# Weight conversion from float64 words: the sign bits as a 16-bit operation into ScalarE's word, and the opening lists re-laid

## Chip, core and metric

The kernel runs on one core of a Trainium2 chip. The metric is the device time of one execution, in microseconds (us). The engines that matter here are TensorE (PE in the profile, PEld for its weight loads), VectorE (DVE), ScalarE (ACT) and the SP queue, which issues every DMA.

## The reference

An attention between 512 tokens and 32 state rows per head is followed by a feed-forward layer over 4608 rows. The two weight matrices arrive as float64, the rest as float32.

```python
scores = scale * np.matmul(x, state.transpose(0, 1, 3, 2))      # B, H, S, Ns, D = 8, 8, 512, 32, 64
a = softmax(scores); xread = np.matmul(a, state)
scores2 = scale * np.matmul(state, x.transpose(0, 1, 3, 2))
a2 = softmax(scores2); sread = np.matmul(a2, x)
x = concat([xread, sread], axis=2) -> (4608, 512)
h = x @ w_in            # 512 x 2048, float64
g = h - np.tanh(h)
return (g @ w_out).astype(np.float32)      # 2048 x 512, float64
```

## The kernel before

The weights are loaded as pairs of 32-bit words and turned into float32 on the chip. `Weight.steps` (L142) makes four steps of a block of 128x512: step 0 on DVE takes the upper word, shifts it left by 3 and masks it (L151); step 1 on DVE ORs the two top bits of the upper word into it, a two-source operation (L152); step 2 on ACT scales the lower word by 2^-29 to an integer `r` (L154); step 3 on DVE adds the two integers (L155). There are 32 blocks: 8 column blocks and 8 quarter blocks of `w_in`, and 16 row blocks of `w_out`.

Sixteen of the blocks belong to the opening. There every engine follows a list written out by hand (`lines`, L897), one token per step: a letter for the operation (`ops`, L861) and a number for its block. Letters a, b, r, p are steps 0, 1, 2, 3 of a `w_in` column block; u, v, w, y are the same of a `w_out` block. S is a score product, c its copy out of PSUM on ACT, T its transpose on DVE, M, B, E, Z, I, J, N, A the rest of the softmax (maximum, subtraction, exponential, sum, epsilon, reciprocal, product, transpose back). m is the product of a `w_in` block with the state, k and R its copies on ACT, e a second product of that kind, h and H the two halves of a hidden block of the first two batches, X its tanh (ACT), L the subtraction (DVE), G and g its high and low part, O and Q the output products. D is a blank matmul that computes nothing that is used. A token starts after the one ahead of it on its engine and after the tokens it needs: h needs A0, H needs A1 for the first pair, m needs p, e needs T and c of both halves.

Behind the opening the steps `convert_win` and `convert_wout` (L569, L274) run the other 16 blocks, gated behind the tanh steps, with an order that the framework's scheduler plans from its own costs. `r` lies in a tile of 512 integers with two buffers (tag "cr" for `w_in`, "s" for `w_out` in the opening).

The loads stand in one list on the SP queue (L609 to L620): head, xT, the first `w_in` block w00d, xT, half of `sps`, the second block w01d, the other half of `sps`, `sp4`, and behind them two halves of xT for the third score product and the rest of the weights. The first token, a0, needs w00d; the first state product, m0, needs p0 and both halves of `sps`.

Of the kernel before, what the change touches and what calls it, by code (L numbers as in the profile page):

```python
# [8 lines left out]
F32 = mybir.dt.float32  # L9
F32R = mybir.dt.float32r  # L10
U32 = mybir.dt.uint32
I32 = mybir.dt.int32
ALU = mybir.AluOpType
AF = mybir.ActivationFunctionType
# [28 lines left out]
def attention_ffn(ctx: ExitStack, tc: tile.TileContext, early, xT, xn, bh, sm, sl, win, wout, xout, sout):  # L43
# [10 lines left out]
    nc = tc.nc  # L54
# [71 lines left out]
    class Weight:  # L126
# [5 lines left out]
        def load(self):  # L132
            if self.src.dtype == F32:
                self.raw = next(raws)(f"{self.name}d", [P, 512], F32)
                dst = self.raw
            else:
                self.raw = next(raws)(f"{self.name}d", [P, 512, 2], U32)
                dst = self.raw.rearrange("p f w -> p (f w)")
            src = self.src.bitcast(dst.dtype)
            loadlog.append(nc.sync.dma_start(dst, src).ins)  # L140

        def steps(self, dst, tag="cr"):  # L142

            if self.src.dtype == F32:
                return [lambda: None] * 3 + [lambda: nc.gpsimd.tensor_copy(dst, self.raw)]
            low, high = self.raw[:, :, 0], self.raw[:, :, 1]
            u, i = dst.bitcast(U32), dst.bitcast(I32)
            r = pool.tile([P, 512], I32, tag=tag, name=f"{self.name}r", bufs=CB)
            return [

                lambda: nc.vector.tensor_scalar(u, high, 3, 0x3FFFFFFF, ALU.logical_shift_left, ALU.bitwise_and),  # L151
                lambda: nc.vector.scalar_tensor_tensor(u, high, 0xC0000000, u, ALU.bitwise_and, ALU.bitwise_or),  # L152

                lambda: nc.scalar.activation(r, low, AF.Copy, scale=2.0**-29),  # L154
                lambda: nc.vector.tensor_add(i, i, r),  # L155
            ]

        def convert(self, dst):
            for step in self.steps(dst):
                step()  # L160


    SCH = json.loads('{"conv": [8, 8, 9, 9, 11, 11, 12, 12], "pair": [10, 10, 13, 13], "a0": [96, 97], "att2": [12, 13, 13, 23, 27, 28, 29], "att3": [36, 39, 40, 41, 43, 44, 45, 49, 50], "att4": [49, 53, 53, 55, 57, 59, 60], "att5": [70, 73, 74, 75, 76, 78, 79, 83, 84], "att6": [83, 86, 87, 88, 90, 91, 92], "att7": [102, 105, 106, 107, 108, 110, 111, 116, 117], "m0": [19, 19, 19, 22, 22, 22, 22, 25, 25, 28, 28, 28, 30, 30, 30, 36], "m1": [50, 51, 54, 58, 61, 62, 67, 68, 77, 80, 82, 85], "wo": [8, 12, 12, 13, 13, 16, 19, 22], "r1": [99, 100, 103, 104], "at0": [10, 16], "plain": [1, 5, 6, 7]}')
# [390 lines left out]
    def advance(units, n=1):  # L554
# [7 lines left out]
    w0 = [  # L562
        [Weight(win[4 * q + r], f"w0{4 * q + r}" if q < 2 else f"w{q}{r}") for r in range(4)]
        for q in range(NQ)
    ]
# [75 lines left out]
    def rows(q, j):  # L641
        return q[:, :, (j % 4) * P : (j % 4) * P + P]
# [73 lines left out]
    def win_step(n):  # L716
        def run(j):
            if j not in csteps:
                if j // 2 not in wb:
                    tag, bufs = ("wf", WB) if j < 4 else (f"mr1{j // 2}", 1)  # L720
                    wb[j // 2] = pool.tile([P, 2, 512], F32, tag=tag, name=f"w00{j}", bufs=bufs)
                csteps[j] = wcols[j].steps(wb[j // 2][:, j % 2], "cr")
            csteps[j][n]()
            if n == 3:
                nc.sync.dma_start(rows(wf[j // 4], j), wb[j // 2][:, j % 2].rearrange("p (r f) -> p r f", r=4))
        return run

    def wout_step(n):
        def run(f):
            if f not in wsteps:  # L730
                if f < WHOLE_ROWS:
                    if f % 2 == 0:
                        whole.append(pool.tile([P, 2, 512], F32, tag=("mr", "stage")[f // 2], name=f"wor{f}", bufs=(RRB, SB)[f // 2]))
                    worows[f] = whole[f // 2][:, f % 2]
                else:
                    worows[f] = pool.tile([P, 512], F32, tag="wor", name=f"wor{f}", bufs=RB)
                wsteps[f] = wos[f].steps(worows[f], "s")
            wsteps[f][n]()
            if n == 3:
                with ExitStack() as gates:  # L740
                    for x in stores:
                        gates.enter_context(tc.issue_after(x))
                    load(int(f < len(ring)))
        return run
# [32 lines left out]
    def keep(k):  # L777
        def run(j):
            nc.scalar.copy(m_both[j // 4][:, k, :, (j % 4) * P : (j % 4) * P + P], mps[j][k][:, :2])
        return run  # L780
# [77 lines left out]
    def halt(t):  # L858
# [4 lines left out]
        "W": (late_scores, "S"), "U": (late_turn, "TW"),  # L863
        "B": (sub_max, "M"), "E": (exp, "B"), "Z": (sums, "E"), "I": (add_eps, "Z"),
        "J": (invert, "I"), "N": (normalize, "J"), "A": (turn_back, "N"),
        "a": (win_step(0), ""), "b": (win_step(1), "a"), "r": (win_step(2), ""), "p": (win_step(3), "br"),
        "u": (wout_step(0), ""), "v": (wout_step(1), "u"), "w": (wout_step(2), ""), "y": (wout_step(3), "vw"),
        "i": (wout_high, "y"), "l": (wout_low, "i"), "m": (product, "p"), "k": (keep(0), "m"), "R": (keep(1), "m"),
        "h": (hidden_half(0), "k"), "H": (hidden_half(1), "hR"), "X": (tanh, "H"), "L": (sub_tanh, "X"),
        "G": (g_high, "L"), "g": (g_low, "G"), "O": (output_part((0, 1)), ""), "Q": (output_part((2, 3)), "O"),  # L870
# [19 lines left out]
    for j in range(2, 8):  # L890
        more[f"r{j}"] = f"p{j - 2}"
        more[f"w{j}"] = f"y{j - 2}"
        if j - 2 >= WHOLE_ROWS:
# [2 lines left out]

    lines = {  # L897
        "PE": (
            "D0 D0 D0 S0 W0 D0 D0 D0 D0 S1 D0 D0 m0 e0 D0 D0 m1 S2 h0 h1 H0 e1 H1 m2 O0 h2 Q0 H2 O1 m3 Q1 h3 "
            "O2 H3 m4 Q2 h4 m5 H4 O3 h5 Q3 H5 m6 O4 h6 Q4 H6 O5 m7 Q5 h7 O6 H7 Q6 h8 h9 H8 O7 H9 Q7"  # L900
        ),
        "DVE": (
# [4 lines left out]
        ),  # L907
        "ACT": (
# [3 lines left out]
        ),  # L912
# [23 lines left out]
    a0 = state_read(0, [ss[0], ss[1]])  # L936
# [3 lines left out]
    m1 = [m_units(g) for g in range(2)]  # L940
# [7 lines left out]
    steps = [(0, f) for f in range(HALF)] + [(1, f) for f in range(NFF)] + [(0, f) for f in range(HALF, NFF)]  # L948
    steps += [(i, f) for i in range(2, B + 1) for f in range(NFF)]
    for st, (i, f) in list(enumerate(steps))[HALF:]:  # L950
        with ExitStack() as gates:
            for x in tanhs[st + (st < 2 * NFF)]:
# [8 lines left out]
        if st + LAG < len(steps):  # L961
            ni, nf = steps[st + LAG]
            if nf % 4 == 0:
                if (ni, nf) == (B, 0):
                    advance(turn)
                with ExitStack() as gates:
                    for x in tanhs[st + 1] if st < 2 * NFF else ():
                        gates.enter_context(tc.issue_after(x))
                    chunks[ni].prepare(nf // 4, tanhs[st - 2] if st >= 2 * NFF else ())
            chunks[ni].hidden(nf)  # L970
# [6 lines left out]
        with ExitStack() as gates:  # L977
# [6 lines left out]
            for b in range(2, B):  # L984
                n = SCH[f"att{b}"].count(st)
# [67 lines left out]
```

## Time and profile before

| what | us |
|---|---|
| median of 3 runs (lowest to highest) | 641.0 (640.27 to 641.15) |
| the profiled execution's own time | 641.2 |
| span of the core in that execution | 639.4 |
| PE busy | 634.3 |
| DVE busy | 440.3 |
| ACT busy | 347.6 |

The span is what the trace covers; the execution takes 1.8 us more, which lies around it. Busy times are sums over an engine's instructions, and the instructions of one engine overlap by their start-up, so an engine that is busy for the whole of a stretch has no idle time in it, and the step from one start to the next is shorter than an instruction's duration.

### The profile page before, as it was taken

The page shows a single profiled execution, that of the slowest core. Times are in us where ns is not written, and L with a number is a line of the kernel's source. Part 1 is how long each engine was busy: PE and PEld are TensorE (multiplying, and loading weights), DVE is VectorE, ACT ScalarE, POOL GpSimd, SP SyncE. Part 2 cuts the span into 40 slices and gives each one's busy share as a digit, 9 for nine tenths or more (in the row PEclk, how much of TensorE's full clock was granted, in tenths as well). Part 3 has the DMA queues.
Part 4 walks back from the last instruction along what each step waited for, and adds up shares of the span by engine and source line. Part 5 has one row for each costly group of instructions (what it writes and reads, how often), then busy time and mean ns, then how long its engine had stood idle before and what let it go on. Part 6 is the DMA issues. An engine that isn't in the chain of part 4 may idle for free.

```text
span 639.4 us, 10251 instructions
## 1 busy us (share of the span) xinstructions
PE 634.3 (99%) x3828; PEld 504.8 (79%) x3828; DVE 440.3 (69%) x757; ACT 347.6 (54%) x630; POOL 0.3 (0%) x5
## 2 busy tenths in 40 slices
PE   8999999999999999999999999999999999999998
PEld 5456867888888788878888788878888788888897
DVE  6999999898683874688553686486664875453442
ACT  4865768777674543756553466445543453342442
POOL 0000000000000000000000000000000000000000
PEclk9999999999999999999999999999999999999999
DMA  8993889267886335543533236773361233221400
GB/s 318 401 319 134 281 290 351 85 207 238 261 264 182 104 98 199 174 136 118 171 115 111 83 95 202 251 288 94 121 198 46 79 108 124 76 66 34 133 33 34
DMA packets 66738, 105.87 MB, mean 166 GB/s; under 512 B 12288, under 2 KB 32640, under 8 KB 66688
## 3 DMA queue, kind: packets, MB, share of 16 engines
q1 hardware_dynamic: 66688, 105.21, 50.2%
q8 instruction: 30, 0.49, 0.3%
q14 instruction: 20, 0.16, 0.1%
HBM read 69.01 MB, written 35.65 MB: 164 GB/s over the span
## 4 chain that ended last, share of the span: by engine, by line
PE 97%; DVE 1%; DMA 1%; issue 0%; SPq 0%; ACT 0%
PE ops L519 19%; PE ops L520 19%; PE ops L521 19%; PE hps L472 10%; PE hps L473 9%; PE hps L474 9%; PE hps L812 3%; PE mps L219 2%; PE mps L756 1%; PE rps L410 1%; PE ops L838 1%; PE mps L218 1%; DMA w00d<-in_win 1%; PE sps L287 1%; DVE w L155 0%; DVE z L696 0%
## 5 line engine op out<-in xcount | busy, mean ns | idle before, releaser
L519 PE MATMUL ops<-wo,g 128*128 128x512 f32 x534 | 211.9, 399 | 0.0
L520 PE MATMUL ops<-wo,g 128*128 128x512 f32 x534 | 208.2, 390 | 0.0
L521 PE MATMUL ops<-wo,g 128*128 128x512 f32 x534 | 198.0, 390 | 0.0
L480 DVE TENSOR_TENSOR t<-hps,t 128x512 f32<-128x512 f32 (+1 forms) x134 | 87.7, 656 | 114.6 <-ACT t L480 114.1
L480 ACT ACTIVATE t<-hps 128x512 f32<-128x512 f32 (+1 forms) x134 | 76.5, 573 | 145.3 <-PE hps L474 144.4
L519 PEld LDWEIGHTS ops<-wo,g 128*128 128x128 f32 x534 | 100.2, 188 | 26.9 <-issue 4.2
L520 PEld LDWEIGHTS ops<-wo,g 128*128 128x128 f32 x534 | 100.3, 188 | 22.6 <-issue 2.3
L521 PEld LDWEIGHTS ops<-wo,g 128*128 128x128 f32 x534 | 100.0, 188 | 21.8 <-DVE t L480 0.8
L124 DVE TENSOR_TENSOR g<-t,g 128x512 fp32r<-128x512 f32 (+1 forms) x134 | 87.4, 656 | 32.4 <-ACT g L123 30.3
L123 ACT CAST g<-t 128x512 fp32r<-128x512 f32 (+1 forms) x134 | 79.7, 596 | 48.9 <-DVE t L480 40.4
L472 PE MATMUL hps<-aT,m 128*128 128x512 f32 x232 | 90.7, 391 | 0.0
L473 PE MATMUL hps<-aT,m 128*128 128x512 f32 x232 | 90.4, 390 | 0.0
L474 PE MATMUL hps<-aT,m 128*128 128x512 f32 x232 | 89.8, 389 | 0.0
L472 PEld LDWEIGHTS hps<-aT,m 128*128 128x128 f32 x232 | 43.5, 188 | 10.8 <-DVE wor L151 0.8
L473 PEld LDWEIGHTS hps<-aT,m 128*128 128x128 f32 x232 | 43.6, 188 | 9.6 <-issue 0.8
L474 PEld LDWEIGHTS hps<-aT,m 128*128 128x128 f32 x232 | 43.5, 188 | 9.1
L124 DVE TENSOR_TENSOR wst<-w,wst 64x512 fp32r<-64x512 f32 (+1 forms) x56 | 36.3, 648 | 4.7 <-ACT wst L123 3.1
L124 DVE TENSOR_TENSOR m<-mr,m 128x1024 fp32r<-128x1024 f32 x29 | 35.4, 1222 | 6.0 <-ACT m L123 5.6
L123 ACT CAST m<-mr 128x1024 fp32r<-128x1024 f32 x29 | 30.4, 1047 | 8.8 <-DVE mr L252 5.7
L220 ACT COPY st<-mps 128x512 f32<-128x512 f32 (+1 forms) x56 | 29.9, 558 | 8.7 <-PE mps L219 4.2
L123 ACT CAST wst<-w 64x512 fp32r<-64x512 f32 (+1 forms) x56 | 32.8, 586 | 0.7
L812 PE MATMUL hps<-at,mr 128*128 128x512 f32 x40 | 20.1, 600 | 0.1
(237 smaller groups left out, 588.0 us busy)
## 6 DMA issues: line engine op xcount, KB each, us to landing
md<-st SPq DMA_DIRECT2D x96, 128.0 KB, 2.8
mr<-md SPq DMA_DIRECT2D x20, 512.0 KB, 4.2
xn<-in_xn SPq DMA_DIRECT2D x16, 512.0 KB, 6.0
out_x<-ob SPq DMA_DIRECT2D x30, 256.0 KB, 2.7
xT<-in_xT SPq DMA_DIRECT2D x12, 512.0 KB, 4.7
w<-wf SPq DMA_DIRECT2D x12, 512.0 KB, 4.7
pd<-pe SPq DMA_DIRECT2D x16, 256.0 KB, 2.1
p2t<-pd SPq DMA_DIRECT2D x64, 64.0 KB, 2.0
```

Of the source, the lines that this page charges most:

```text
L123: nc.scalar.copy(hi, src)
L124: return (sub or nc.vector).tensor_sub(lo, src, hi)
L219: nc.tensor.matmul(ps, s[:, 0, h], t[:, e], start=(g == 1), stop=True)
L220: nc.scalar.copy(stage[:, e], ps)
L472: nc.tensor.matmul(ps, mhi[k][:, cols], ahi[:, k], start=(k == 0), stop=False)
L473: nc.tensor.matmul(ps, mhi[k][:, cols], alo[:, k], start=False, stop=False)
L474: nc.tensor.matmul(ps, mlo[k][:, cols], ahi[:, k], start=False, stop=(k == nk - 1))
L480: tanhs.append((nc.scalar.activation(t, ps, AF.Tanh).ins, nc.vector.tensor_sub(t, ps, t).ins))
L519: nc.tensor.matmul(o, g[:, 0, tok], wo[f][:, 0, cols], start=first, stop=False)
L520: nc.tensor.matmul(o, g[:, 0, tok], wo[f][:, 1, cols], start=False, stop=False)
L521: return nc.tensor.matmul(o, g[:, 1, tok], wo[f][:, 0, cols], start=False, stop=last).ins
L812: nc.tensor.matmul(hps[n], m[:, k], ats[b][k], start=(k == 0), stop=(k == 1))
```

## The change

Step 1 becomes a one-source operation on 16-bit elements: it takes the top 16 bits of the float64 (every fourth 16-bit element of the raw tile), keeps the two top bits, and writes them into the upper half of each word of `r`, which ACT has filled with a number of at most 4 bits. Step 3 is unchanged; it adds `r`, which now holds both parts. So step 1 needs step 2 (ACT) and no longer step 0, and step 3 needs steps 0 and 1. `convert` runs the steps in the order 0, 2, 1, 3.

The opening lists change too: two blank matmuls behind S1 go; on DVE Z0 stands ahead of T1, the softmax of the first two halves is interleaved anew, and b5 comes later; on ACT c1 stands ahead of r1 and f0 ahead of E1.

```diff
+            top = self.raw.rearrange("p f w -> p (f w)").bitcast(U16).rearrange("p (f w) -> p f w", w=4)[:, :, 3]
+            carry = r.bitcast(U16).rearrange("p (f w) -> p f w", w=2)[:, :, 1]
             return [
                 lambda: nc.vector.tensor_scalar(u, high, 3, 0x3FFFFFFF, ALU.logical_shift_left, ALU.bitwise_and),
-                lambda: nc.vector.scalar_tensor_tensor(u, high, 0xC0000000, u, ALU.bitwise_and, ALU.bitwise_or),
+                lambda: nc.vector.tensor_scalar(carry, top, 0xC000, None, ALU.bitwise_and),
                 lambda: nc.scalar.activation(r, low, AF.Copy, scale=2.0**-29),
                 lambda: nc.vector.tensor_add(i, i, r),
             ]
         def convert(self, dst):
-            for step in self.steps(dst):
-                step()
+            steps = self.steps(dst)
+            for n in (0, 2, 1, 3):
+                steps[n]()
...
-        "a": (win_step(0), ""), "b": (win_step(1), "a"), "r": (win_step(2), ""), "p": (win_step(3), "br"),
-        "u": (wout_step(0), ""), "v": (wout_step(1), "u"), "w": (wout_step(2), ""), "y": (wout_step(3), "vw"),
+        "a": (win_step(0), ""), "b": (win_step(1), "r"), "r": (win_step(2), ""), "p": (win_step(3), "ab"),
+        "u": (wout_step(0), ""), "v": (wout_step(1), "w"), "w": (wout_step(2), ""), "y": (wout_step(3), "uv"),
...
         "PE": (
-            "D0 D0 D0 S0 W0 D0 D0 D0 D0 S1 D0 D0 m0 e0 D0 D0 m1 S2 h0 h1 H0 e1 H1 m2 O0 h2 Q0 H2 O1 m3 Q1 h3 "
+            "D0 D0 D0 S0 W0 D0 D0 D0 D0 S1 m0 e0 D0 D0 m1 S2 h0 h1 H0 e1 H1 m2 O0 h2 Q0 H2 O1 m3 Q1 h3 "
...
         "DVE": (
-            "T0 U0 M0 a0 B0 b0 p0 T1 a1 M1 b1 B1 Z0 p1 I0 Z1 J0 I1 N0 J1 A0 N1 a2 A1 b2 u0 a3 v0 p2 y0 u1 L0 v1 L1 y1 "
-            "u2 a5 v2 b5 y2 u3 b3 v3 p3 l2 L2 p5 T2 g2 y3 a4 u4 b4 v4 p4 y4 a7 l3 b7 L3 p7 l4 g3 u6 u5 a6 v5 L4 b6 "
+            "T0 U0 M0 a0 B0 b0 p0 Z0 T1 a1 M1 b1 B1 I0 p1 J0 N0 Z1 I1 A0 J1 a2 N1 b2 A1 u0 p2 v0 a3 y0 L0 u1 v1 L1 y1 "
+            "u2 a5 v2 y2 u3 b3 v3 p3 l2 L2 b5 T2 p5 g2 y3 a4 u4 b4 v4 p4 y4 a7 l3 b7 L3 p7 l4 g3 u6 u5 a6 v5 L4 b6 "
...
         "ACT": (
-            "c0 r0 E0 r1 c1 R0 n0 k0 E1 f0 s0 t0 n1 R1 r2 k1 f1 c3 w0 c2 r3 X0 w1 s1 t1 X1 r4 n2 k2 w2 R2 f2 w3 i2 "
+            "c0 r0 E0 c1 r1 R0 n0 k0 f0 E1 s0 t0 n1 R1 r2 k1 f1 c3 w0 c2 r3 X0 w1 s1 t1 X1 r4 n2 k2 w2 R2 f2 w3 i2 "
```

## Rows read from the trace of the kernel before

**Rows 1.** The page: busy time by engine, and the chain that ended last

```profile
PE 634.3 (99%) x3828; PEld 504.8 (79%) x3828; DVE 440.3 (69%) x757; ACT 347.6 (54%) x630; POOL 0.3 (0%) x5
PE 97%; DVE 1%; DMA 1%; issue 0%; SPq 0%; ACT 0%
```

**Rows 2.** Windows: stretch, its length, busy us (instructions) by engine, clock, DMA

```profile
7.80:16.66 8.86, 7.57 (x189) 4.54 (x188) 8.69 (x19) 6.06 (x14) 0.00 (x0) 1.00 1.04 407
16.66:66.00 49.34, 49.34 (x423) 29.19 (x424) 47.70 (x89) 34.58 (x72) 0.00 (x0) 1.00 0.82 283
66.00:102.00 36.00, 36.00 (x203) 26.03 (x202) 34.42 (x62) 24.41 (x44) 0.00 (x0) 1.00 0.86 306
...
150.00:300.00 150.00, 150.00 (x803) 122.27 (x802) 104.73 (x176) 88.89 (x157) 0.00 (x0) 1.00 0.56 172
```

**Rows 3.** Waits of PE's weight loads after 16.7 us: total, times, longest

```profile
PEld hps L812 <- DVE at L714: 1.4, 2, 1.0
```

**Rows 4.** Timeline, DVE: start, us, line, operation [idle before <-releaser]

```profile
7.83 0.43 DVE L151 TENSOR_SCALAR w<-w00d 128x512 uint32<-128x512 uint32 x1 [0.81 <-DMA w00d<-in_win]
...
8.77 0.69 DVE L152 SCALAR_TENSOR_TENSOR w<-w00d,w 128x512 uint32<-128x512 uint32 x1
9.60 0.69 DVE L155 CUSTOM_DVE_ANT_0 w<-w,w00r 128x1024 uint16<-128x1024 uint16 x1
10.29 0.72 DVE L679 STREAM_TRANSPOSE e<-sps 128x512 f32<-128x512 f32 x1
...
14.90 0.24 DVE L702 RECIPROCAL z<-z 128x16 f32<-128x16 f32 x1
...
15.95 0.67 DVE L714 STREAM_TRANSPOSE at<-e 128x512 f32<-128x512 f32 x1
...
17.44 0.70 DVE L714 STREAM_TRANSPOSE at<-e 128x512 f32<-128x512 f32 x1
```

**Rows 5.** Timeline, ACT

```profile
5.47 0.37 ACT L669 COPY s<-sps 128x256 f32<-128x256 f32 x1 [3.46 <-DVE e L677]
...
8.89 0.63 ACT L692 ACTIVATE e<-e 128x512 f32<-128x512 f32 x1 [0.39 <-DVE e L689]
10.85 0.69 ACT L154 ACTIVATE w01r<-w01d 128x512 int32<-128x512 uint32 x1 [1.33 <-DMA w01d<-in_win]
11.42 0.58 ACT L672 COPY s<-sps 128x512 f32<-128x512 f32 x1
```

**Rows 6.** Timeline, PE and PEld; the last row is from the chain, in order of time

```profile
10.18 1.14 PE L648 MATMUL warm<-blank 128*128 128x256 f32 x4
11.24 1.16 PE L756 MATMUL mps<-w,sps 64*32 64x128 f32 x64
...
15.45 1.12 PE L287 MATMUL sps<-xT,bdr 64*32 64x512 f32 x15
16.66 2.84 PE L812 MATMUL hps<-at,mr 128*128 128x512 f32 x6
...
16.66 0.30 PEld L812 LDWEIGHTS hps<-at,mr 128*128 128x128 f32 x2 [1.01 <-DVE at L714]
...
106.23 1.02 PE sps L287 x16
```

**Rows 7.** Lines L151 and L152: ns min/median/max, first and last start

```profile
L151 DVE TENSOR_SCALAR wor<-wo5d x2: 420/420/420, 39.5 to 39.9; 128x512 uint32<-128x512 uint32 x2
L152 DVE SCALAR_TENSOR_TENSOR wor<-wo5d,wor x2: 673/678/682, 40.5 to 44.9; 128x512 uint32<-128x512 uint32 x2
```

**Rows 8.** Windows of L152 alone: stretch, its length, DVE busy (instructions)

```profile
7.80:66.00 58.20, 10.67 (x16) 1.00 0.86 301
```

**Rows 9.** Lines L152 and L154, one block of the planned part

```profile
L152 DVE SCALAR_TENSOR_TENSOR wor<-wo8d,wor x1: 687/687/687, 68.8 to 68.8; 128x512 uint32<-128x512 uint32 x1
L154 ACT ACTIVATE wo8r<-wo8d x1: 673/673/673, 70.8 to 70.8; 128x512 int32<-128x512 uint32 x1
```

**Rows 10.** Windows, around PE's idle stretch in the opening

```profile
8.00:9.20 1.20, 0.03 (x2) 0.04 (x2) 1.20 (x3) 0.81 (x2) 0.00 (x0) 1.00 1.04 411
```

More of the change, by code (lines that the diff above doesn't have):

```diff
@@ L11 @@
 U32 = mybir.dt.uint32
+U16 = mybir.dt.uint16
 I32 = mybir.dt.int32
```

## The prediction

> **What bounds the kernel now.** I read the page's busy times and its chain first. PE is busy for 634.3 of 639.4 us and makes 97% of the chain that ended last [rows 1], so a time is saved only where PE waits. The windows say where that is: from 7.80 to 16.66 us PE is busy for 7.57 of 8.86 us, and some of that is blank matmuls; from 16.66 us on it is busy for all of 49.34, of 36.00 and of 150 us, at a granted clock of 1.00 [rows 2]. The list of waits agrees: after 16.7 us the weight loads' waits for another engine that reach PE come down to the start of h0 and H0, which wait for DVE's transposes A0 and A1 [rows 3]. A busy PE could still hide a pause inside an instruction's modelled end; the steps from start to start behind 16.66 us show none beyond the changes between fp32 and fp32r products, which stay. DVE is busy too in the opening, 47.70 of 49.34 us [rows 2], and that is the trap: a full engine, but nobody on the chain waits for it.
>
> So the question is when h0 and H0 start, and whether anything behind them begins to wait. Before, DVE's first conversion began at 7.83 us, when w00d landed; A0 ran from 15.95 to 16.62 and A1 from 17.44 to 18.14 us [rows 4]; h0 began at 16.66 us [rows 6]. The six instructions of h0, h1 and H0, two each, take 2.84 us [rows 6]: a step of 0.53, four of 0.43, and 0.60 for the last one's own length. So H0's first began at 16.66 + 0.53 + 3 x 0.43 = 18.48 us, 0.34 after A1's end: A0 alone held PE.
>
> **The change part by part.**
>
> *The price of the new step 1.* The trace has no 16-bit operation with gaps. The nearest rows are L151, one source, the same 8-byte step on its input, 0.42 us, and L152, which it replaces, 0.68 us [rows 7]. In steps from start to start these are 0.34 and 0.60 us (a0 at 7.83 is followed at 8.17, b0 at 8.77 has room for 0.60 before the next). I take 0.34, because L151 is the same kind of instruction with the same source step, and only the width and the gap of the output differ. The fastest bound is L155, which passes 1024 contiguous 16-bit elements in 0.69 [rows 4], 0.34 per 512; the slow bound is L152's 0.60, and twice that if a half word has to be merged into its word. At 0.34 each conversion saves 0.26 us of DVE, 16 times in the opening [rows 8], 4.2 us; behind H0 all of it is covered by PE's own queue and is worth nothing.
>
> [...]
>
> *To A0.* I follow DVE's new list with the old steps. b0 starts at 8.77 as before (r0 on ACT began when w00d landed and needs 0.69, as r1 did [rows 5], so it is done by 8.52); it ends at 9.19, and p0 starts at about 9.3 instead of 9.60 [rows 4]. Z0 now comes next (E0 ended at 9.52 [rows 5]), then T1 at 10.5, 0.2 later than before. Now the new wait: ACT's copy c1 stands ahead of r1, and ACT's copy of a score bank waits for DVE's transpose of it, as c0 did for T0 [rows 5]. So c1 starts at 11.25 when T1 ends, r1 at 11.73 instead of 10.85, and is done at 12.42. DVE reaches b1 at about 12.1 and stands there until 12.45; queued behind it are B1, I0, p1 and the whole softmax. After b1 0.34, B1 0.60, I0 0.08, p1 0.59, J0 (0.24 to its end, [rows 4]), N0 0.60, Z1 0.68 to its end and I1 0.12, A0 starts at 15.75 and ends at 16.42, 0.20 earlier than before. h0 also needs S2: sixteen such products take 1.02 us [rows 6], S2 starts at 15.45 [rows 6], so h0 starts at 16.49, a gain of 0.17.
>
> *To H0.* Between A0 and A1 there were N1 and a2; now there are J1 (0.16), a2 (0.34), N1 (0.57) and b2 (0.34). From A0's start 15.75 plus its step 0.59, A1 starts at 17.75 and ends at 18.45, 0.31 later than before. H0, ready by PE's own pace at 16.49 + 0.53 + 3 x 0.43 = 18.31, waits for it until 18.49. That is when it started before. The 0.17 us won at h0 are given back at H0; the sum is 0.0, with 0.1 either way for the hand-off times.
>
> *The blanks.* Two blanks (four instructions, 1.06 us, 10.18 to 11.24 [rows 6]) go, worth nothing: m0 needs the second half of `sps`, which stands behind w01d in the SP queue, and w01d landed only at 10.8 (r1 waited for it until 10.85 [rows 5]). So m0 still starts at about 11.2. If that cover were gone, m0 could start at 10.1, but m1 and S2 further on wait for p1 and for their own data, not for m0.
>
> *The rest.* p1 ends at about 14.2, before m1, which starts some 1.1 us (m0's length [rows 6]) ahead of S2. From m2 on every conversion is ready earlier than before, because DVE has less to do; b5's later place (behind l2 and L2, two steps of 0.6) costs nothing, as p5 follows it at once and m5 stands six products down PE's list. In the planned part the saving is again DVE's alone, and step 1 now waits for ACT (rival 3). No DMA is moved on the SP queue. Sum against the profiled execution: 639.4 + 0.0 = 639.4 us of span and 641.2 us of time; this stands 0.2 above the median of the runs, so the forecast in terms of the median is 641.0.
>
> **The rivals.**
>
> 1. *The new step 1 runs at L152's pace, so that it saves nothing.* Speaking for it: the output goes to half words with gaps. Then b0, b1 and b2 are each 0.26 longer on the way to A1 and H0 starts at 19.27: +0.8 us, 641.8. Behind it DVE has its old load, which PE did not wait for.
>
> 2. *The stream is slower than that (slower than before).* At a step of 0.90 us, half as much again as L152, three conversions on the way to A1 cost 3 x 0.56 = 1.7 us, and then DVE, which is full from 16.66 to 66 us [rows 2], becomes PE's bound: the other 13 conversions of the opening add 13 x 0.30 = 3.9. Together 5.6 us, 646.6; at 1.20 some 10 us, 651. The point at which this decides is about 0.70 us a step. [...] Against it stands L151's row.
>
> 3. *DVE is blocked in the planned part.* Of wo8, step 1 on DVE started at 68.8, but ACT's step 2 at 70.8 and ended at 71.5 [rows 9]. With the new order step 1 waits for that, 2.7 us at worst, and tanh subtractions and low parts that PE needs are queued behind it. The planner will place step 1 later, and DVE has 1.6 us idle in that stretch [rows 2] besides what the change saves there, so I expect it absorbed. If one such block isn't, PE loses up to 2.7 us less the lead that the low parts have: about +1.5 us, 642.5.
>
> 4. *The clock falls.* Without the blanks PE idles from about 10.2 to 11.2 us, after an idle 8.0 to 9.2. In that first stretch PE was busy for 0.03 of 1.20 us with a granted clock of 1.00 [rows 10], so one pause was not enough; two, nearly back to back, were not seen. [...]
>
> 5. *A gain above 0.2%.* It needs 1.3 us. h0 can't start before S2's data and products allow (16.49), so the opening gives at most 0.2; the rest would have to come from a luckier plan, but sixteen fp32 score products between two groups of fp32r products take 1.02 us in all [rows 6], and the number of such groups is fixed; only what it costs to change over can be saved, a part of that each time.
>
> **How the numbers follow.** About 0.2%, 1.3 us, is what a measurement of this kernel can tell from no change. Forecast (641.0, with 640.5 to 641.5 of its own): 0.70. Rival 1: 0.13. Rivals 2, 3 and 4: 0.05, 0.05 and 0.04. Rival 5: 0.03. Within 0.2% are the forecast and rival 1, 0.83; slower 0.14; faster 0.03. The range 640.2 to 642.1 holds the forecast and rival 1 with the spread of the runs, and leaves out the rest.
>
> **What would show it.** In the profile of the changed kernel: step 1 at about 0.42 us (0.68 is rival 1, more is rival 2); c1 at about 11.3 and r1 behind it, and an idle DVE of 0.3 to 0.4 us ahead of b1, ended by ACT; A0 ending near 16.4 and A1 near 18.45; H0, not h0, as the place where PE waits; m0 still at 11.2; DVE's busy time down by about 32 x 0.26 = 8 us, and PE still full from H0 on. The forecast is wrong if PE shows waits behind 20 us, a clock under 1.00, or if T1 or c1 turns out not to hold r1 (then A1 comes 0.4 earlier, a gain of 0.2).

## The result, and the profile after

The changed kernel takes 645.1 us (median of 6 runs, 644.59 to 645.83) where the kernel before took 641.1 in runs on the same chip (640.27 to 641.5). The ratio is 1.0059, with a 95% interval of 1.0047 to 1.0071: 3.0 to 4.6 us slower. The profiled execution took 645.56 us, its span is 643.7; that is 4.3 us more span than before. All ratios here and below leave out two runs that were much longer than the others of their kernel, one of the five of `c1_torn_by_hand` (1294.9 us) and one of the 27 of the kernel before beside it (704.6 us).

The page after: busy times by engine [answers rows 1]. The chain that ended last is PE's for 97%, as before.

```profile
PE 638.1 (99%) x3824; PEld 504.3 (78%) x3824; DVE 433.5 (67%) x757; ACT 348.0 (54%) x630; POOL 0.3 (0%) x5
```

DVE is relieved by 6.8 us (440.3 to 433.5), as the change says. But PE, whose products are the same but for two blanks less, is busy for 3.8 us *more* (634.3 to 638.1). So time wasn't lost in waiting for something; PE's own work became longer. The windows say where [answers rows 2, same columns]:

```profile
16.66:66.00 49.34, 49.32 (x422) 28.89 (x423) 44.55 (x89) 34.29 (x71) 0.00 (x0) 1.00 0.83 281
66.00:102.00 36.00, 36.00 (x182) 25.11 (x181) 31.30 (x61) 23.37 (x40) 0.00 (x0) 1.00 0.85 292
```

The granted clock (third column from the end) is 1.00 here, and the page shows a 9 (90% or more) for it in every slice. From 66 to 102 us PE is full in both kernels, but it ran 203 instructions there before and 182 after. The count alone doesn't say that instructions became dearer: 16 of the 21 belong to a group of fp32 products that now stands behind 102 us. It says that PE's order changed, and that the groups of fp32 products between the fp32r products are the place to read. The timeline of PE, the fp32 groups alone (start, us, line, operation; sixteen instructions are one group). First the kernel before:

```profile
80.95 1.09 PE L756 MATMUL mps<-w,sps 64*32 64x512 f32 x16
86.29 1.09 PE L756 MATMUL mps<-w,sps 64*32 64x512 f32 x16
94.81 1.09 PE L756 MATMUL mps<-w,sps 64*32 64x512 f32 x16
100.37 1.09 PE L756 MATMUL mps<-w,sps 64*32 64x512 f32 x16
106.17 1.09 PE L287 MATMUL sps<-xT,bdr 64*32 64x512 f32 x16
```

The same after the change:

```profile
85.76 1.09 PE L760 MATMUL mps<-w,sps 64*32 64x512 f32 x16
91.10 1.06 PE L760 MATMUL mps<-w,sps 64*32 64x512 f32 x8
92.98 1.06 PE L760 MATMUL mps<-w,sps 64*32 64x512 f32 x8
98.06 1.06 PE L760 MATMUL mps<-w,sps 64*32 64x512 f32 x8
99.71 1.06 PE L760 MATMUL mps<-w,sps 64*32 64x512 f32 x8
103.67 1.09 PE L760 MATMUL mps<-w,sps 64*32 64x512 f32 x16
109.46 1.06 PE L291 MATMUL sps<-xT,bdr 64*32 64x512 f32 x8
110.89 1.06 PE L291 MATMUL sps<-xT,bdr 64*32 64x512 f32 x8
```

Five groups became eight: three were torn into halves of eight, with output products in between, and a half takes as long as a whole (1.06 against 1.09). What one torn group costs is read from PE's steps from start to start. After, around one half:

```profile
90.78 0.39 PE L524 MATMUL ops<-wo,g 128*128 128x512 f32 x1
91.10 1.06 PE L760 MATMUL mps<-w,sps 64*32 64x512 f32 x8
92.09 0.50 PE L525 MATMUL ops<-wo,g 128*128 128x512 f32 x1
92.42 0.39 PE L523 MATMUL ops<-wo,g 128*128 128x512 f32 x1
```

Here L523 to L525 are output products, L472 and L473 hidden products of the planned part; both are fp32r. A step between two of them is 0.23. Into the group it is 0.32 (90.78 to 91.10), the group holds PE for 0.99, and the step out of it is 0.33. So a half group costs 0.09 + 0.99 + 0.10 = 1.18 us beyond the output products, and two halves 2.36. A whole group before, by the same reading:

```profile
94.49 0.39 PE L473 MATMUL hps<-aT,m 128*128 128x512 f32 x1
94.81 1.09 PE L756 MATMUL mps<-w,sps 64*32 64x512 f32 x16
95.82 0.50 PE L472 MATMUL hps<-aT,m 128*128 128x512 f32 x1
96.16 0.39 PE L473 MATMUL hps<-aT,m 128*128 128x512 f32 x1
```

That is 0.09 + 1.01 + 0.11 = 1.21. One torn group adds 1.15 by this reading, three of them 3.45. The same can be read from a stretch that holds all five groups and nothing of the opening: from the last hidden products of the opening's lists to the first group of score products behind the five. Their rows, before and then after:

```profile
62.21 1.02 PE L812 MATMUL hps<-at,mr 128*128 128x512 f32 x2
...
211.66 1.09 PE L287 MATMUL sps<-xT,bdr 64*32 64x512 f32 x16
```

```profile
62.48 1.02 PE L816 MATMUL hps<-at,mr 128*128 128x512 f32 x2
...
215.43 1.09 PE L291 MATMUL sps<-xT,bdr 64*32 64x512 f32 x16
```

149.45 us before, 152.95 after: +3.50, three times 1.17. In both kernels PE runs 716 instructions in it, the same number of each shape, and has no idle time, so only the order differs. Ahead of it lie +0.27 us, and behind it the 0.5 that is left of the 4.3, which wasn't followed. I call the stretch "62 to 211" below; scatter in the opening can't touch it.

### The profile page after: what moved, and what is told of

Same layout as the page of the kernel before. It is cut to its first block, busy times and chain, and to the rows that moved or that the text cites. A ratio compares the mean times of both kernels' runs of the same rounds, so it can differ in the third digit from the quotient of the medians.

```text
span 643.7 us, 10234 instructions
## 1 busy us (share of the span) xinstructions
PE 638.1 (99%) x3824; PEld 504.3 (78%) x3824; DVE 433.5 (67%) x757; ACT 348.0 (54%) x630; POOL 0.3 (0%) x5
## 4 chain that ended last, share of the span: by engine, by line
PE 97%; DVE 1%; DMA 1%; ACT 0%; SPq 0%; issue 0%
PE ops L523 19%; PE ops L525 19%; PE ops L524 19%; PE hps L476 9%; PE hps L478 9%; PE hps L477 9%; PE hps L816 3%; PE mps L223 2%; PE mps L760 2%; PE rps L414 1%; PE ops L842 1%; PE sps L291 1%; PE mps L222 1%; DMA w00d<-in_win 1%; DVE w L158 0%; DVE z L700 0%
## 5 line engine op out<-in xcount | busy, mean ns | idle before, releaser
L523 PE MATMUL ops<-wo,g 128*128 128x512 f32 x534 | 211.8, 399 | 0.0
L525 PE MATMUL ops<-wo,g 128*128 128x512 f32 x534 | 201.3, 391 | 0.0
L523 PEld LDWEIGHTS ops<-wo,g 128*128 128x128 f32 x534 | 100.3, 188 | 26.4 <-issue 3.4
L525 PEld LDWEIGHTS ops<-wo,g 128*128 128x128 f32 x534 | 100.1, 188 | 25.0 <-issue 1.7
```

Of the source, the lines that this page charges most:

```text
L523: nc.tensor.matmul(o, g[:, 0, tok], wo[f][:, 0, cols], start=first, stop=False)
L525: return nc.tensor.matmul(o, g[:, 1, tok], wo[f][:, 0, cols], start=False, stop=last).ins
```

## The experiments

Three theories stood against each other. **P**: PE loses 1.17 us for each group that the planned order tears, and nothing else matters. **O**: the re-laid opening costs the time. **W**: DVE, whose step 1 now waits for ACT, is blocked in the planned part.

### Which half of the change: opening or planned part

`e1_old_planned`: the new opening, the old conversion behind it (the code is shown against the changed kernel).

```diff
-        def steps(self, dst, tag="cr"):
+        def steps(self, dst, tag="cr", old=False):
...
-            steps = self.steps(dst)
-            for n in (0, 2, 1, 3):
+            steps = self.steps(dst, old=True)
+            for n in (0, 1, 2, 3):
```

> New opening and new step 1 there; the 16 blocks of the planned part keep the old two-source step 1 and the old order of steps. Theory P (the planner tore three groups of sixteen fp32 products into two halves of eight, 1.17 us each, and nothing else costs): five whole groups again, 641.1 to 641.4 us, 3.5 to 4 below the changed kernel. Rival O (the re-laid opening, its blanks or its waits cost the time): 645. Rival W (DVE waits for ACT in the planned part): 641.3 as well, this run does not part it from P.

`e2_new_planned`: the kernel before, with the new step 1 and the new order in `convert` alone.

```diff
-            for step in self.steps(dst):
-                step()
+            steps = self.steps(dst, new=True)
+            for n in (0, 2, 1, 3):
+                steps[n]()
```

> Old opening with the old step 1; new step 1 and the order 0, 2, 1, 3 only in the 16 blocks of the planned part. Theory P: three torn groups, +3.5, 644.6 us. Rival O: 641.1, as the opening is the old one. Rival W: 644.6 too.

Measured: `e2_new_planned` 644.90 us, ratio 1.0057 (1.0042 to 1.0072), 3.7 us; `e1_old_planned` 642.87, ratio 1.0021 (1.0011 to 1.0032), 1.3 us. In the trace `e2_new_planned` has the same three torn groups, and its stretch 62 to 211 is 3.51 longer than before; that of `e1_old_planned` is 0.01 longer, with five whole groups. So the planned part alone brings the loss, and O falls as its main cause. That the opening alone took 1.3 us was above what I expected of it; more on that below.

### Is it the tearing, the wait for ACT, or the price?

`q1_two_source_on_r`, with the new opening, keeps the old two-source operation and its price in the planned part, but lets it work on ACT's word, so that it waits for ACT. `t0_no_act_wait`, with the old opening, has a price near the new one (0.42 us) and no wait for ACT; it leaves out the two top bits in the planned part. Both cuts show step 1 there against the kernel before.

```diff
-                lambda: nc.vector.scalar_tensor_tensor(u, high, 0xC0000000, u, ...),
+                lambda: nc.vector.scalar_tensor_tensor(r.bitcast(U32), high, 0xC0000000, r.bitcast(U32), ...),
```

> New opening; in the planned part step 1 is a two-source operation again (old price), but ORs the two top bits into ACT's word, so it waits for ACT as the new one does. The planned order on PE has one torn group. Theory P: 641.3 + 1.2 = 642.5 us. Rival W: the wait for ACT is there at a higher price on DVE, so 645 or more. Rival O: 645.

```diff
-                lambda: nc.vector.scalar_tensor_tensor(u, high, 0xC0000000, u, ...),
+                lambda: nc.vector.tensor_scalar(u, u, 0x3FFFFFFF, None, ALU.bitwise_and),
```

> The opening of before; in the planned part step 1 is a one-source 32-bit operation at the new price that waits for nothing but step 0, in the old order (it leaves out the two top bits of the upper word in those 16 blocks). In the planned order no group is torn. Theory P: the time of before, 641.0 to 641.6, although DVE has as little to do as with the change. If the lower price alone were enough to change the plan for the worse, more.

`t0_no_act_wait` gave 641.74 us where before gave 641.71, ratio 1.0004 (0.9992 to 1.0015); five whole groups, and 62 to 211 takes 149.45 us, to the hundredth the length of before:

```profile
62.30 1.02 PE L817 MATMUL hps<-at,mr 128*128 128x512 f32 x2
...
211.75 1.09 PE L292 MATMUL sps<-xT,bdr 64*32 64x512 f32 x16
```

`q1_two_source_on_r` gave 643.59, ratio 1.0039 (1.0024 to 1.0055); one group is torn, and 62 to 211 is 1.35 longer (1.17, and 0.24 in a pause inside another group). Its whole time is a microsecond more than I expected: PE also waited 0.9 us near 485 us for a load, and the opening was 0.64 late. So a lower price by itself tears nothing, a wait for ACT (with the order 0, 2, 1, 3 that goes with it) at the old price tears one group, and both together three.

How a wait for ACT can tear a group is seen on ACT, whose L189 (L185 before) copies a group's two banks out of PSUM. Its timeline in the kernel before, and then after:

```profile
82.13 0.59 ACT L185 COPY mr<-mps 128x512 f32<-128x512 f32 x1 [1.79 <-PE mps L756]
82.62 0.62 ACT L123 CAST g<-t 128x512 fp32r<-128x512 f32 x1
83.14 0.59 ACT L185 COPY mr<-mps 128x512 f32<-128x512 f32 x1
```

```profile
86.94 0.59 ACT L189 COPY mr<-mps 128x512 f32<-128x512 f32 x1 [0.41 <-PE mps L760]
88.87 0.68 ACT L157 ACTIVATE w33r<-w33d 128x512 int32<-128x512 uint32 x1 [1.34 <-DMA w33d<-in_win]
89.45 0.67 ACT L157 ACTIVATE wo9r<-wo9d 128x512 int32<-128x512 uint32 x1
90.00 0.59 ACT L189 COPY mr<-mps 128x512 f32<-128x512 f32 x1
```

Before, the two copies stand 1.0 us apart. After, the planner has put two of ACT's step 2, on which DVE now waits, between them, and the first of these waits for a load. The second bank comes free 3 us after the first, and PE's order has one half of the next group first (91.10), three output products, and then the other half (92.98). Both copies had ended by 90.6, so in this execution PE waited for neither: what tears the group is the planned order. The second torn group has the same picture (copies at 92.92 and 96.69, a step 2 between them). The third has not: its copies stand 1.0 us apart (105.44 and 106.44) with a cast between, like the pair at 82.13 that was followed by a whole group. So it is with the torn groups of `t1_one_torn` and `t2_two_torn` below; and in `q1_two_source_on_r` a whole group follows a pair of copies that has a step 2 between (96.22 and 98.04). So a step 2 between the copies fits two of the three torn groups, and why the planner tears a group isn't shown.

### The dose

Four more kernels put 0, 1 or 2 torn groups into the planned order. All have the opening of before. `t1_one_torn` is `e2_new_planned` with ACT's step 2 at a higher priority for the planner, `t0_none_torn` adds one wait that holds the halves of the score group together, `t2_two_torn` has the new step in the `w_in` blocks alone. `c1_torn_by_hand` is the kernel before, its conversion unchanged, in which the second half of two groups is made to wait for ACT's copy of the first half's bank.

```diff
+                if n in (2,):
+                    with tc.high_priority(offset=40):
+                        steps[n]()
```

> The same without the added wait: the opening of before, the new step 1 in the planned part with ACT's step 2 at a higher priority. In the planned order one of five groups of sixteen fp32 products is torn, that of the scores. Theory P: 1.17 us above before, 642.3 to 642.8. Theory W: about +3 us, 644 to 645.

```diff
+                for x in freed if b == 2 else ():     # ACT's copies of the banks ahead
+                    tc.add_manual_dep(one, x.name, ...)
```

> The opening of before (lists and conversion); in the planned part the new step 1 for all 16 blocks, in the new order, but ACT's step 2 gets a higher priority with the planner, and the score products of half three also wait for the two ACT copies ahead of them. In the planned order no group of sixteen fp32 products is torn. Theory P (each torn group costs PE 1.17 us and nothing else changed): the time of before, 641.1 to 641.6, five groups of 1.02 to 1.09 us. Theory W (the new step 1 makes DVE wait for ACT, and PE loses by that): as the kernel with the new planned part, +3 us or more, 644 to 645. If the one added wait bites, PE shows a wait of a microsecond or two ahead of the score products near 106 us.

```diff
-            steps = self.steps(dst, new=True)
-            for n in (0, 2, 1, 3):
+            steps = self.steps(dst, new=new)       # new: w_in alone
+            for n in (0, 2, 1, 3) if new else (0, 1, 2, 3):
```

> The opening of before; in the planned part the new step 1 and the new order for the eight quarter blocks of w_in alone, the old for the eight of w_out. In the planned order two of five groups are torn. Theory P: 2 x 1.17 = 2.3 us above before, 643.4 to 644.0. Theory W: half the blocks wait for ACT, so about half of 3.5, +1.8, but without a whole number of extra groups in the trace.

```diff
+    TORN = ((2, 1), (3, 0))
...
+            for k in (1, 0):
+                for r in reversed(range(4)):
...
+                    if after:
+                        tc.add_manual_dep(one, after.name, ...)
+                after = nc.scalar.copy(torn[:, k], pss[k]).ins
```

> The kernel before with nothing changed in the conversion or the opening; only two of its groups of sixteen fp32 products (second batch of quarter 2, first batch of quarter 3) are torn on purpose: the second half of each waits for ACT's copy of the first half's bank, and output products stand between. In the planned order there are seven groups of fp32 products in place of five. Theory P: 2 x 1.17 = 2.3 us above before, 643.5 to 644.1 where before gives 641.4, with PE busy throughout. Theory W (the loss comes from DVE's wait for ACT, which is not here): the time of before, 641.0 to 641.8.

What the 13 kernels gave; "62 to 211" is that stretch of the profiled execution against 149.45, "timed" the ratio against before on the same chip, in us:

| kernel | extra groups | 62 to 211 | timed (95%) |
|---|---|---|---|
| t0_no_act_wait | 0 | 0.00 | +0.3 (-0.5 to +1.0) |
| o2_new_step_old_lists | 0 | +0.13 | +0.2 (-0.4 to +0.8) |
| e1_old_planned | 0 | +0.01 | +1.3 (+0.7 to +2.1) |
| o1_opening_all | 0 | 0.00 | +1.0 (+0.4 to +1.6) |
| o3_new_lists_old_step | 0 | 0.00 | +1.0 (+0.4 to +1.6) |
| t0_none_torn | 0 | +1.58 | +1.9 (+1.1 to +2.6) |
| d_whole_groups | 0 | +3.71 | +2.1 (+1.2 to +3.1) |
| q1_two_source_on_r | 1 | +1.35 | +2.5 (+1.5 to +3.5) |
| t1_one_torn | 1 | +3.37 | +3.1 (+1.9 to +4.2) |
| t2_two_torn | 2 | +2.34 | +2.6 (+1.7 to +3.5) |
| c1_torn_by_hand | 2 | +2.48 | +3.1 (+2.2 to +4.0) |
| e2_new_planned | 3 | +3.51 | +3.7 (+2.7 to +4.6) |
| after | 3 | +3.50 | +3.8 (+3.0 to +4.6) |

PE runs the same 716 instructions in the stretch in all thirteen. Where it waits for nothing, the stretch grows by 1.17 for each extra group, to within 0.15: 0.00 to 0.13 for none, 2.34 and 2.48 for two, 3.51 for three. `c1_torn_by_hand` shows it without the change: its conversion and its opening are those of before, PE has no idle time in the stretch, and two extra groups cost 2.48. (In its trace four groups lie in halves, not two, but four of these halves meet in pairs, so that there are seven groups.) W in the form of a blocked DVE doesn't explain that, and DVE's waits for step 2 in the planned part of the changed kernel are two of 0.4 us between 60 and 110 us.

By their times alone not all of this could be told: `t1_one_torn` with 644.6 us came out where W had put it and 2 us above P, and `c1_torn_by_hand` with 3.1 us lies above P's 2.3, which its interval just holds. It is the traces that tell them apart.

P missed in `t0_none_torn` and `t1_one_torn`. The first has five whole groups and was still 1.9 us slower; I had expected nothing. Its loss is at one place, and `t1_one_torn` has the same one, beside a shorter wait at 97 us. The timeline of ACT and PE there, in `t0_none_torn`:

```profile
177.11 1.05 ACT L124 CAST m<-mr 128x1024 fp32r<-128x1024 f32 x1 [4.13 <-DMA mr<-md]
178.06 0.58 ACT L228 COPY st<-mps 128x512 f32<-128x512 f32 x1
178.12 0.39 PE L484 MATMUL hps<-aT,m 128*128 128x512 f32 x1
178.69 0.50 PE L226 MATMUL mps<-wst,sms 128*128 128x512 f32 x1 [0.19 <-ACT st L228]
179.03 0.40 PE L227 MATMUL mps<-wst,sms 128*128 128x512 f32 x1
180.16 0.47 PE L529 MATMUL ops<-wo,g 128*128 128x512 f32 x1 [0.73 <-ACT st L228]
```

ACT stood for 4.13 us in front of a cast whose load had not landed, the copy of a bank was queued behind it, and PE stood for want of the bank: 178.12 to 180.16 are three steps, 2.04 us in place of 0.68, which is 1.36 of the 1.58. These two kernels are also the only ones in which ACT's step 2 was given a higher priority. `e2_new_planned`, which has the same new step without that, has no idle PE in the stretch, and neither has the changed kernel. So this wait can't be put down to the new step 1 by itself; the raised priority is the likelier cause, but no run has it alone. What P has wrong is "nothing else matters": an order without torn groups can still hold a wait. In the changed kernel the stretch grew by the torn groups alone.

`d_whole_groups` is the changed kernel with each group made to wait for both copies ahead of it.

```diff
+                for x in after:                      # ACT's copies of both banks
+                    tc.add_manual_dep(one, x.name, ...)
```

> The changed kernel whole, with one thing added: in the planned part the products of a pair, and the first planned score products, also wait for the two ACT copies that free the two banks before them, so that both halves of a group become ready at one time. New step 1 and its wait for ACT stay in all 32 blocks. Theory P: five whole groups, 641.2 to 641.5 us. Rival W: the wait for ACT is still there, so 645. Rival O: 645.

It gave 643.61 us, ratio 1.0033 (1.0018 to 1.0048). All five groups are whole, and P had said 641.2 to 641.5. But the added wait bit in the profiled execution, the slowest of the nine: PE stood 2.1 us at 97.5, and lost more behind it (see the last section). It is no clean test of P; it only shows that holding the halves together by a wait can cost as much as the tearing (3.71 us in the stretch against 3.50).

### What the opening costs

`o1_opening_all` is `e1_old_planned` again; `o2_new_step_old_lists` takes from it the new step 1 alone, with the old lists (b5 moved behind L2); `o3_new_lists_old_step` the lists alone. The planned part is that of before in all three.

> Once more the whole new opening (lists and conversion) with the planned part of before; five whole groups. Theory P with the trace of the changed kernel (PE reached 62.94 us where before reached it at 62.67): 0.3 above before, 641.5 to 641.9. Theory O (the opening costs about as much as the first run of this kernel showed): 1.0 to 1.6 above before.

> Opening: the new step 1 with the lists of before (b5 alone is moved behind L2, since it now waits for r5); planned part of before. From the working of the prediction: every b is 0.2 to 0.26 us shorter, A0 and H0 come some 0.3 us earlier, S2 holds h0 at 16.5: 0.1 to 0.2 us below before, within its scatter. Theory O in the form that the 16-bit step costs something: above before by 0.5 or more.

> Opening: the new lists with the step 1 of before; planned part of before. Three longer steps (0.25 us each) stand ahead of A1, which the lists put 0.3 us later, so H0 comes at about 19.3 to 19.5 in place of 18.5: +0.8 to +1.0 us against before. If the lists cost nothing but the place of A1, this and the run with the old lists add up to the whole opening.

The new step alone changed nothing that can be measured (1.0003, 0.9994 to 1.0012). The lists cost 1.0 us with either step (1.0016, 1.0007 to 1.0025). The traces are clear on the first 20 us if they are read from the landing of w00d, that is from the start of a0, which lies anywhere from 6.7 to 8.4 us in these executions. In six kernels with the old lists and the old step (that is without `c1_torn_by_hand`, where w01d was the later one) A0 starts 8.09 to 8.12 us behind a0 and A1 9.58 to 9.62. In `o2_new_step_old_lists` a0 starts at 7.30, A0 at 15.15 and A1 at 16.65: 7.85 and 9.35, both 0.25 earlier. With lists and step new A0 stands at 7.89 to 7.91 in all five executions and A1 at 9.86 to 9.88 in four of them: A0 about 0.21 earlier, A1 0.27 later. The old step on the new lists (`o3_new_lists_old_step`) gives 8.08 and 10.31. From a0 to the row of the opening's last hidden products (62.21 before) it is 54.38 us before, 54.44 after and in `o1_opening_all`, 54.11 in `o2_new_step_old_lists` and 54.88 in `o3_new_lists_old_step`. So the new step was worth 0.25 us in the opening, and the new lists gave it back.

That leaves most of the timed +1.0 of the lists open. The profiled execution of `o1_opening_all` shows 0.06 for the opening and a wait of 1.1 us far behind it:

```profile
PE rps L415 <- DMA p2t<-pd: 1.1, 1, 1.1
```

A wait at this place shows in other kernels too and not in every execution: with the new lists it was 0.9 us in `q1_two_source_on_r` and 0.5 in `o3_new_lists_old_step`, and 0.2 or less in the other three; with the old lists it was 0.3 in `c1_torn_by_hand` and 0.1 or nothing in the rest. The longer waits are all with the new lists, but a single trace of each kernel can't say that the lists bring them. In the first run of this kernel, `e1_old_planned`, w02d landed about a microsecond late, k1 stood behind r2 on ACT, and A1 came at 18.36; such late transfers hit one kernel or another. Whether the new lists meet them more often wasn't settled. Nor does this microsecond show in the changed kernel: 3.7 us for the planned part (2.7 to 4.6) and 1.0 for the lists would be 4.7, and it lost 3.8 (3.0 to 4.6); the intervals leave room for both.

## Why the prediction was wrong

It said 641.0 and no change; it was 3.8 us slower. The steps in turn:

- *What bounds the kernel.* Right. PE's own work decided the time, and DVE's gain of 6.8 us was worth nothing.
- *The price of step 1.* Right in its neighbourhood. I took 0.42 us a piece and 0.34 a step; it is 0.45 to 0.48, and 0.35 a step, and DVE's busy time fell by 6.8 us and not by 8:

```profile
12.61 0.47 DVE L155 TENSOR_SCALAR w01r<-w01d 128x512 uint16<-128x512 uint16 x1 [0.32 <-ACT w01r L157]
12.96 0.68 DVE L693 TENSOR_TENSOR e<-e,m 128x512 f32<-128x512 f32 x1
```

  Rivals 1 and 2 fall: they put the step at 0.60 and 0.90 us, and here it is 0.35 (12.61 to 12.96).

- *To A0, to H0, and the new wait.* Right. c1 stood ahead of r1, and DVE waited 0.32 for r1 (0.3 to 0.4 was said; the row above). A0 was said to come 0.20 earlier and A1 0.31 later; counted from a0 they came 0.23 earlier and 0.26 later. The terms after b1 add up to 15.70 for A0 and not to the 15.75 written; that would be 0.25 earlier, and the difference is within the 0.1 allowed for hand-offs. H0, not h0, held PE. These are c1, A0, A1 and the wait that answers rows 3:

```profile
11.42 0.59 ACT L676 COPY s<-sps 128x512 f32<-128x512 f32 x1 [1.69 <-DVE e L683]
...
15.93 0.70 DVE L718 STREAM_TRANSPOSE at<-e 128x512 f32<-128x512 f32 x1
...
17.91 0.70 DVE L718 STREAM_TRANSPOSE at<-e 128x512 f32<-128x512 f32 x1
...
PEld hps L816 <- DVE at L718: 1.8, 2, 1.0
```

- *The blanks.* Right in the sum: m0 began earlier (10.38, where 11.2 was said), but its second half waited for `sps` until 11.38, and the clock stayed at 1.00. Rival 4 did not come.
- *The rest.* This is the step that failed: "In the planned part the saving is again DVE's alone." The planned part is no fixed list: here a cheaper step 1 on DVE that waits for ACT changed the order that the planner gave to ACT and PE as well. PE's own work, put at no change, grew by 3.50 us between 62 and 211 us. I had the right question in rival 3, the wait for ACT in the planned part, and priced it as a wait on DVE (2.7 us at worst, "The planner will place step 1 later"). The planner did place things elsewhere, among them ACT's step 2 between the copies on which two of the three torn groups depend, and it issued the halves of three groups apart. How it comes to that stays open.
- *Rival 5.* It says of the changes between fp32 and fp32r products that "the number of such groups is fixed", as the first paragraph says that they "stay", and used this against a gain only. The number went from five to eight, 1.17 us for each of the three. Nor does the charge at such a change go with the types, as that rival and my first paragraph have it: it goes with the tile's shape (0.09 us more with the type unchanged and nothing more from fp32r to fp32 at one shape, last section). The row of such a group stood in my text with its 1.02 us; what was missing was the question what half of it costs.

The chance of 0.14 for slower was too small for a reason that can be named: I priced moved instructions where the order is written out, and took the rest of the kernel, whose order is worked out anew at every edit, for unchanged. What that order can cost PE shows in the trace of the changed kernel: 0.99 us for a half group against 1.01 for a whole one before, with 0.09 and 0.10 us at its two changes of shape.

## What to carry to other kernels

Where a planner orders part of a kernel, an edit to an engine off the critical path is an edit to the order on the critical engine too: after the edit, compare that engine's order first (how many groups, how many changes of tile shape), before any time is added up. Take a stretch in which PE is full and runs the same instructions in both kernels; if it is longer after, look for groups that run in halves, each of which takes as long as a whole one (0.99 against 1.01 us here), and for changes of tile shape (about 0.1 us each here). And compare stretches between two landmarks that every version shares, since a late first load moves everything behind it (a0 started anywhere from 6.7 to 8.4 us here) and hides a tenth of a microsecond under half a one.

## What the runs showed of the hardware

- Eight fp32 products of 64x32 that all read one half of the 128 partitions take as long as sixteen that read both: 0.99 against 1.01 us. In `c1_torn_by_hand` the halves of two different groups that met in PE's order at 101.5 us took together the time of one group (1.09 us).
- Each change between the 128x128 products and the 64x32 ones costs about 0.1 us on the way in (0.32 for a step of 0.23) and as much on the way out (0.33). The kernel before tells that this goes with the shape and not with the type, because the hidden products of its opening (L812) and its first output products (L838) are fp32 and of 128x128:

```profile
24.43 1.02 PE L812 MATMUL hps<-at,mr 128*128 128x512 f32 x2
25.29 1.88 PE L838 MATMUL ops<-wor,t 128*128 128x512 f32 x4
...
34.61 0.40 PE L521 MATMUL ops<-wo,g 128*128 128x512 f32 x1
34.84 1.02 PE L812 MATMUL hps<-at,mr 128*128 128x512 f32 x2
35.79 0.67 PE L756 MATMUL mps<-w,sps 64*32 64x128 f32 x32
```

  Two such products take 0.86 us when products of their own type and shape follow (24.43 to 25.29), and 0.95 when fp32 products of 64x32 follow (34.84 to 35.79): 0.09 more with the type unchanged. From fp32r to fp32 at one shape the step is 0.23 (34.61 to 34.84), as between two fp32r products. On the way out, an fp32 product of 128x128 behind fp32 products of 64x32 takes 0.53 (at 39.43) in place of 0.43, again with the type unchanged.
- In `d_whole_groups` PE stood for 2.1 us, and then the granted clock fell from 1.00 to a mean of 0.57 over 4 us. Windows of that execution, columns as in rows 2:

```profile
96.00:98.00 2.00, 1.51 (x7) 0.92 (x5) 1.84 (x4) 1.11 (x3) 0.00 (x0) 1.00 1.12 378
98.00:100.00 2.00, 0.39 (x8) 0.18 (x16) 1.88 (x4) 1.97 (x5) 0.00 (x0) 1.00 0.97 348
100.00:104.00 4.00, 4.00 (x24) 2.52 (x9) 1.91 (x3) 2.13 (x4) 0.00 (x0) 0.57 1.04 392
104.00:108.00 4.00, 4.00 (x30) 2.38 (x29) 3.04 (x6) 3.66 (x8) 0.00 (x0) 1.00 1.03 393
```

  From 100 to 104 us PE was busy for all of the time; 24 instructions went through where the next 4 us at 1.00, groups included, took 30. In the opening of the kernel before PE stood for 1.2 us [rows 10] at a clock of 1.00. So this wait of 2.1 us cost more than its length: the stretch 62 to 211 grew by 3.71, with all groups whole.
